# Two feed-forward layers begun at the last block of tokens, one more sweep by seven products, and subtractions lent from VectorE to GpSimd

## The chip, the cores and the metric

One core of a Trainium2 chip runs the whole program. The metric is the device time of one execution in microseconds (us), as the median of the runs. The engines are TensorE (PE; its weight loads are PEld), VectorE (DVE), ScalarE (ACT) and GpSimd (POOL); SyncE (SP) issues nearly all DMA transfers.

## The reference

Windowed attention with a distance bias, then two feed-forward layers on the 2304 tokens:

```python
rel = pos[:, None] - pos[None, :]
scores = scale * np.matmul(q, k.transpose(0, 1, 3, 2))       # 4 x 8 heads, 576 tokens, 64 wide
scores = np.where((rel >= 0) & (rel < 128), scores - slopes * abs(rel), -1e9)
x = softmax(scores) @ v                                       # then 2304 tokens x 512
h = x @ w_in                                                  # 512 x 2048
x = np.where(h > 0, h, np.exp(np.minimum(h, 0)) - 1) @ w_out  # layer 0, ELU
h = x @ w_in2
out = (h / (1 + np.exp(-h))) @ w_out2                         # layer 1, SiLU
```

## The kernel before

**Stages.** Attention runs first, in units of 256 tokens and two heads, and in between them the first sweep of layer 0 (`block_first`, on blocks of 256 or 512 tokens): a sweep is a quarter of the 2048 hidden columns, for both products. The last such block (`block_first(NB - 1)`) stands alone behind the attention, from about 181.5 us on. Then come 21 steps: a step is one layer, one sweep and one of three blocks of 768 tokens. Steps 0 to 8 are sweeps 1 to 3 of layer 0, steps 9 to 20 the four sweeps of layer 1. The results add up in the tiles `acc0` to `acc2`, one a block.

**Precision.** Every operand is held as two float32r tiles, a rounded upper half (ScalarE copies it) and a lower half (VectorE subtracts the upper from the value), and a product is three matmuls: upper by upper, upper by lower, lower by upper.

**Seven products.** The first product of every step (`quad`) takes 2 x 2 blocks by seven products, not eight. Its operands are combinations of x, in the tiles `c0` to `c6`, and of the weights, in `wa` to `wd`. The combinations of x are made by VectorE's `form` operations and the halves, once a block (`make`), are stored to DRAM (`d`) and reloaded (`reload`) in the later sweeps. The results are summed into the tiles `hs` and `h2` (a "sum" is such an instruction), go through the activation in the tiles `e`, `xs`, `t2` and `t3`, and land as upper and lower halves in the tiles `g`. The second product goes by eight products (`outputs`, 96 matmuls of 384 columns a step of layer 0) or by seven (`seven_outputs`, 84), where `BY_SEVEN` lists the layer and sweep; by seven, `seven_activated` forms combinations of the activated tiles and `place` makes their halves, and `y_weight` makes those of the weights `w1` and `yb`.

**Which block comes first.** `ORDER` lists the blocks of each sweep, with block 0 first in sweep 1. Its combinations and those of block 1 are made during the attention (`make_ahead`, through the staging tiles `st`), while those of block 2, whose tokens are attended last, are made during step 1, for step 2.

**The order of the work** is a planner's (`Plan`): every operation has a cost and a latest start worked back from due times, and at build time the planner runs through the program and emits each engine's queue in that order. An engine then works its queue strictly in order. In the planner, VectorE and GpSimd share a port: an operation of the one with all operands in SBUF keeps the other's out, while VectorE's operations on PSUM are free (`port=False`).

```python
    ORDER = ((0, 1, 2), (2, 1, 0), (0, 1, 2)), ((0, 1, 2), (2, 1, 0), (0, 1, 2), (2, 1, 0))
    BY_SEVEN = {(0, 2), (1, 0), (1, 1), (1, 2), (1, 3)}
    HELP = {"place": (0, 1), "lower": (0, 1), "wlow": (0, 1), "c": (0, 1)}
```

By `HELP`, none of each kind of lower half goes to GpSimd, and in the layers it has nothing to do.

Of the kernel before, what the change touches and what calls it, by code (L numbers as in the profile page):

```python
# [13 lines left out]
AF = mybir.ActivationFunctionType  # L14
# [8 lines left out]
def f32(ap):  # L23
    return ap.bitcast(F32)
# [10 lines left out]
class Plan:  # L35
# [14 lines left out]
    def add(self, eng, cost, fn, r=(), w=(), due=1.0e9, moved=0, after=(), floor=0.0, port=None, kind=None):  # L50
        op = Op(eng, cost, fn, due, moved and self.DMA_START + self.DMA_END + moved / self.DMA_RATE or self.DRAIN.get(eng, 0.0), len(self.ops))
        op.moved, op.floor, op.kind = moved, floor, kind
# [84 lines left out]
def attention_elu_silu_kernel(  # L137
# [195 lines left out]

    def split_weight(tag, keys, src, half, w, r, low_eng="DVE"):
# [4 lines left out]
        eng = {"DVE": nc.vector, "POOL": nc.gpsimd}[low_eng]  # L339
        add(low_eng, cost if low_eng == "DVE" else 1.1,  # L340
            lambda: eng.tensor_tensor(T[lo], f32(src()), f32(T[hi]), op=ALU.subtract), r=list(r) + [hi], w=[lo])

# [3 lines left out]
    def y_weight(t):  # L346
# [18 lines left out]
        def form(d, x, y):  # L365
            add("DVE", 0.34, lambda: nc.vector.tensor_tensor(d[0](), x[0](), y[0](), op=ALU.subtract), r=x[1] + y[1], w=d[1])
        src, r = whole(t, 1)
# [10 lines left out]
    def weight(i):  # L378
# [48 lines left out]
        else:  # L427
# [625 lines left out]
    ns = {"hs": 0, "h2": 0, "e": 0, "g0": 0, "g1": 0, "below": 0, "a": 0}  # L1053
    g_of, g_unread = {}, {}
# [12 lines left out]
    vec = {"DVE": nc.vector, "POOL": nc.gpsimd}
    HELP = {"place": (0, 1), "lower": (0, 1), "wlow": (0, 1), "c": (0, 1)}
    helped = {n: 0 for n in HELP}

    def helper(name):
        a, n = HELP[name]
        helped[name] += a
        if helped[name] >= n:
            helped[name] -= n
            return "POOL"
        return "DVE"

    def place(k, q, i, src, sk):
# [46 lines left out]
    def activated(k, f, half, src, sk):  # L1126
# [9 lines left out]
        if layer == 1:  # L1136
            add("ACT", 0.42, lambda: nc.scalar.activation(T[ek], src(), AF.Silu), r=[sk], w=[ek])
            add("ACT", 0.44, lambda: nc.scalar.activation(T[gk[0]], src(), AF.Silu), r=[sk], w=[gk[0]])
        elif slot("below", 2):
            def bent():  # L1140
# [5 lines left out]
            add("ACT", 0.43, lambda: nc.scalar.activation(T[gk[0]], T[ek], AF.Copy), r=[ek], w=[gk[0]])  # L1146
        else:
            add("ACT", 0.42, lambda: nc.scalar.activation(T[ek], src(), AF.Exp), r=[sk], w=[ek])
            add("DVE", 0.28, lambda: clamp(T[ek]), w=[ek])
            add("DVE", 0.475, lambda: nc.vector.tensor_tensor(T[ek], src(), T[ek], op=ALU.max), r=[sk], w=[ek], port=sk[0] != "m")  # L1150
            add("ACT", 0.43, lambda: nc.scalar.activation(T[gk[0]], T[ek], AF.Copy), r=[ek], w=[gk[0]])
        eng = helper("lower")
        add(eng, 0.475 if eng == "DVE" else 1.0, lambda: vec[eng].tensor_tensor(T[gk[1]], T[ek], f32(T[gk[0]]), op=ALU.subtract),
            r=[ek, gk[0]], w=[gk[1]])

# [229 lines left out]
    def layers():  # L1385
# [85 lines left out]
```

## Time and profile before

| | before |
|---|---|
| time, median of 3 runs | 846.22 us (844.97 to 848.49) |
| the profiled execution | 845.84 us, its span 844.1 us |
| TensorE busy | 833.9 us (99%) |
| VectorE busy | 734.9 us (87%) |
| ScalarE busy | 593.5 us (70%) |
| GpSimd busy | 82.3 us (10%), all before 181.5 us |

The profile is of one execution. Busy time is the union of an engine's instructions, which may overlap on VectorE and ScalarE. The stages named above are the reader's clock: attention up to 181.5 us, the block alone to 203.5, steps 0 to 2 to 297.7, steps 3 to 5 to 386, steps 6 to 8 to 480.2, layer 1 to the end.

### The profile page before, as it was taken

How to read it: one execution, taken by the hardware profiler on the slowest of the kernel's cores; microseconds unless marked ns; L12 is line 12 of the kernel's file. 1: busy time of each engine (PE TensorE's matmuls, PEld its weight loads, DVE VectorE, ACT ScalarE, POOL GpSimd, SP SyncE). 2: the span in 40 equal slices, each digit the busy share in tenths (PEclk: the TensorE clock that was granted, in tenths of full speed). 3: DMA queues.
4: the chain of work that ended last, by engine and by line, in shares of the span. 5: the costliest groups of instructions: out<-in, count | busy, mean ns of one | idle time of the engine just before them, and what ended most of it. 6: DMA issues, size and time to landing. Idle time of an engine off the chain costs nothing.

```text
span 844.1 us, 17025 instructions
## 1 busy us (share of the span) xinstructions
PE 833.9 (99%) x6254; PEld 789.7 (94%) x6254; DVE 734.9 (87%) x1753; ACT 593.5 (70%) x1387; POOL 82.3 (10%) x171
## 2 busy tenths in 40 slices
PE   8999999999999999999999999999999999999998
PEld 5788777778999999999999999999999999999998
DVE  8998997955999869999998789999998899798757
ACT  7988987855876666685857588789757566755532
POOL 6254534410000000000000000000000000000000
PEclk9999999999999999999999999999999999999999
DMA  9765876559817265505786846427661458116722
GB/s 303 253 213 171 268 239 200 191 206 384 311 50 294 81 199 208 217 26 174 286 306 237 281 163 267 166 89 242 245 241 51 149 214 310 50 55 246 286 88 76
DMA packets 75267, 169.66 MB, mean 201 GB/s; under 512 B 5040, under 2 KB 55216, under 8 KB 75184
## 3 DMA queue, kind: packets, MB, share of 16 engines
q1 hardware_dynamic: 74608, 168.05, 56.6%
q8 instruction: 49, 0.80, 0.4%
q10 hardware_dynamic: 576, 0.52, 0.2%
q14 instruction: 34, 0.28, 0.1%
HBM read 126.09 MB, written 42.47 MB: 200 GB/s over the span
## 4 chain that ended last, share of the span: by engine, by line
PE 81%; DMA 7%; DVE 6%; ACT 4%; issue 1%; POOL 1%; SPq 0%; POOLq 0%; ACTq 0%; DVEq 0%
PE m L1176 31%; PE m L1332 25%; PE m L1270 9%; PE m L748 5%; PE m L787 4%; PE a L669 2%; PE s L576 2%; DMA raw<-in_moe_w_in_dram 2%; PE t L636 2%; DMA raw<-in_moe_w_out_dram 2%; DMA d<-xs 1%; ACT p L595 1%; DMA xd<-xt 1%; DMA q<-in_q_dram 1%; DMA acc<-xd 1%
## 5 line engine op out<-in xcount | busy, mean ns | idle before, releaser
L1332 PE MATMUL m<-w,g 128*128 128x256 f32 x1512 | 191.3, 282 | 0.1
L1332 PEld LDWEIGHTS m<-w,g 128*128 128x128 f32 x1512 | 188.7, 190 | 0.3 <-DVE acc L1350 0.3
L1270 PE MATMUL m<-g,w 128*128 128x384 f32 x576 | 110.5, 337 | 1.0 <-DVE e L1144 0.4
L1270 PEld LDWEIGHTS m<-g,w 128*128 128x128 f32 x576 | 101.3, 188 | 2.0 <-DVE e L1144 0.7
L1176 PE MATMUL m<-c,wc 128*128 128x384 f32 x504 | 101.1, 335 | 0.0
L1176 PE MATMUL m<-c,wd 128*128 128x384 f32 x504 | 99.5, 336 | 0.5 <-ACT hs L1185 0.5
L1176 PE MATMUL m<-c,wa 128*128 128x384 f32 x504 | 97.5, 336 | 0.0
L1176 PEld LDWEIGHTS m<-c,wd 128*128 128x128 f32 x504 | 87.9, 188 | 1.1 <-ACT hs L1185 1.1
L1176 PEld LDWEIGHTS m<-c,wc 128*128 128x128 f32 x504 | 88.3, 188 | 0.0
L1176 PEld LDWEIGHTS m<-c,wa 128*128 128x128 f32 x504 | 87.1, 188 | 0.1
L1350 DVE TENSOR_TENSOR acc<-m,acc 128x512 f32<-128x512 f32 (+1 forms) x144 | 75.9, 552 | 8.2 <-PE m L1332 7.0
L617 POOL TENSOR_SCALAR p<-p,sums 128x192 f32<-128x192 f32 x112 | 63.9, 588 | 75.4 <-DVE sums L609 42.8
L595 ACT ACTIVATE p<-p,neg 128x192 f32<-128x192 f32 (+1 forms) x144 | 63.0, 443 | 3.4 <-DVE neg L587 3.4
L1189 DVE TENSOR_TENSOR hs<-m,hs 128x384 f32<-128x384 f32 x84 | 46.5, 554 | 19.5 <-PE m L1176 15.8
L1185 ACT ACTIVATE hs<-m 128x384 f32<-128x384 f32 x84 | 40.8, 486 | 30.1 <-PE m L1176 29.6
L1085 DVE TENSOR_TENSOR g<-xs,g 128x384 fp32r<-128x384 f32 x90 | 49.0, 551 | 7.8 <-ACT g L1083 7.5
L1176 PE MATMUL m<-c,wb 128*128 128x384 f32 x252 | 51.1, 337 | 0.5 <-DVE hs L1189 0.5
L1083 ACT ACTIVATE g<-xs 128x384 fp32r<-128x384 f32 x90 | 45.9, 522 | 3.8 <-DVE xs L1113 2.4
L748 PE MATMUL m<-x,w 128*128 128x512 f32 (+1 forms) x240 | 48.4, 353 | 0.0
L787 PE MATMUL m<-g,w 128*128 128x512 f32 (+1 forms) x240 | 47.2, 350 | 0.6 <-DVE ex L764 0.6
L1332 PE MATMUL m<-g,w 128*128 128x384 f32 x252 | 46.5, 336 | 0.0
L748 PEld LDWEIGHTS m<-x,w 128*128 128x128 f32 x240 | 38.5, 189 | 7.4 <-issue 1.0
(198 smaller groups left out, 1529.6 us busy)
## 6 DMA issues: line engine op xcount, KB each, us to landing
c<-d SPq DMA_DIRECT2D x91, 768.0 KB, 7.3
raw<-in_moe_w_in_dram SPq DMA_DIRECT2D x32, 512.0 KB, 6.8
d<-c SPq DMA_DIRECT2D x21, 768.0 KB, 5.5
raw<-in_moe_w_out_dram SPq DMA_DIRECT2D x28, 512.0 KB, 4.1
d<-st SPq DMA_DIRECT2D x19, 384.0 KB, 3.8
k<-in_k_dram SPq DMA_DIRECT2D x16, 384.0 KB, 5.3
d<-xs SPq DMA_DIRECT2D x14, 384.0 KB, 6.0
v<-in_v_dram SPq DMA_DIRECT2D x18, 256.0 KB, 5.1
```

The costliest lines, as they stand in the source:

```text
L595: nc.scalar.activation(dst, dst, AF.Exp, bias=T["neg", u % 4][:, i:i + 1], scale=-1.0, accum_out=T["sm", u % MS][:, e, j:j + 1])
L617: nc.gpsimd.tensor_scalar(dst, dst, T["sm", u % MS][:, e, j:j + 1], 1.0, op0=ALU.mult, op1=ALU.mult)
L748: nc.tensor.matmul(T[m][:, 0:w], a[:, cs], T["x0", b2][:, c, 0:w], start=(c == 0 and x == 0), stop=(c == NKC - 1 and x == 2))
L787: nc.tensor.matmul(T[m][:, 0:w], a[:, cs], b2[:, 0:w], start=(f == 0 and x == 0), stop=(f == FIRST_F - 1 and x == 2))
L1083: add("ACT", 0.42, lambda: nc.scalar.activation(T[hi], src(), AF.Copy), r=[sk], w=[hi])
L1085: add(eng, 0.475 if eng == "DVE" else 1.0, lambda: vec[eng].tensor_tensor(T[lo], src(), f32(T[hi]), op=ALU.subtract), r=[sk, hi], w=[lo])
L1176: nc.tensor.matmul(T[m][:, 0:HALF], a[:, cs], x[:, j, c, :], start=(begin and c == 0 and n == 0), stop=(c == 1 and n == 2), skip_group_che ...
L1185: add("ACT", 0.4, lambda: nc.scalar.activation(T[s], T[m][:, 0:HALF], AF.Copy), r=[m], w=[s])
L1189: add("DVE", 0.475, lambda: nc.vector.tensor_tensor(T[s], T[m][:, 0:HALF], T[s], op=ALU.add), r=[m], w=[s], port=False)
L1270: nc.tensor.matmul(T[m][:, 0:w], l, rr, start=(f == 0 and x == 0), stop=(f == n - 1 and x == 2))
L1332: nc.tensor.matmul(T[m][:, n * w:(n + 1) * w], l, rr, start=(begin and q == 0 and x == 0 and n == 0), stop=(q == nq - 1 and x == 2 and n = ...
L1350: add("DVE", 0.08 + size / 960.0, lambda: nc.vector.tensor_tensor(dst(), src(), dst(), op=ALU.add), r=[m], w=dk, port=False)
```

## The change

The blocks' order begins with block 2, so its combinations are made at once (`make(0)`, ahead of the last `block_first`), are stored, and blocks 0 and 1 are reloaded in steps 1 and 2. For the second half of x there, `make` uses the tiles `e` and `h2` as well as `xs`. Sweep 1 of layer 0 goes by seven in its second product too. And the planner may move a subtraction from VectorE to GpSimd at build time: one that `either` marks with an alternative cost, if GpSimd is free and VectorE has PSUM work to cover it (`lend`). Also, all activations that go by eight in layer 0 now take the form with one VectorE operation; every second one took a clamp and a maximum.

```diff
+    COVER, SLACK, HURRY = 0.9, 2.0, 1.5
...
     def between(self, a, b):
-        return a.tail + self.LINK if a.eng != b.eng or a.moved else 0.0
+        return a.tail + self.LINK if a.eng != b.eng or a.moved or b.alt else 0.0
+
+    def lend(self, queue, now, busy):
+
+        ready = [x for x in queue if max(x[0], x[1].floor) <= now]
+        alts = [x for x in ready if x[1].alt]
+        free = [x for x in ready if not x[1].port]
+        tied = [x[1].late for x in ready if x[1].port]
+        if not alts or not free and busy <= now:
+            return None
+        x = max(alts, key=lambda x: (x[1].late, x[1].n))
+        if max(busy - now, 0.0) + sum(x[1].cost for x in free) < self.COVER * x[1].alt[0]:
+            return None
+        lead = min([x[1].late for x in ready])
+        if x[1].late < lead + self.SLACK or free and min(tied) < min(x[1].late for x in free) - self.HURRY:
+            return None
+        return x
...
+                if port <= now and free.get("POOL", 0.0) <= now and (x := self.lend(queues.get("DVE", ()), now, free.get("DVE", 0.0))):
+                    queues["DVE"].remove(x)
+                    x[1].eng, x[1].cost, x[1].fn, x[1].tail = "POOL", *x[1].alt, self.DRAIN["POOL"]
+                    x[1].alt, x[1].late = None, -1.0e9
+                    queues.setdefault("POOL", []).append((now, x[1]))
...
-    ORDER = ((0, 1, 2), (2, 1, 0), (0, 1, 2)), ((0, 1, 2), (2, 1, 0), (0, 1, 2), (2, 1, 0))
-    BY_SEVEN = {(0, 2), (1, 0), (1, 1), (1, 2), (1, 3)}
+    ORDER = ((2, 0, 1), (1, 0, 2), (2, 0, 1)), ((2, 0, 1), (1, 0, 2), (2, 0, 1), (1, 0, 2))
+    BY_SEVEN = {(0, 1), (0, 2), (1, 0), (1, 1), (1, 2), (1, 3)}
...
+    LEND = {"wlow": 1.4, "form": 0.75, "place": 1.05, "lower": 1.05, "c": 1.05, "s": 1.05}
+
+    def either(name, cost, fn, r, w):
+
+        if name not in LEND:
+            return add("DVE", cost, lambda: fn(nc.vector), r=r, w=w)
+        part = cost / {"wlow": 0.572, "form": 0.34}.get(name, 0.475)
+        return add("DVE", cost, lambda: fn(nc.vector), r=r, w=w, alt=(LEND[name] * part, lambda: fn(nc.gpsimd)))
...
-            if layer == 0:
+            if layer == 0 and c:
+                own_tiles = [("e", i) for i in range(3)] + [("h2", 1)]
+                src = lambda i, j: T[own_tiles[2 * i + j]]
+                sk = lambda i, j: [own_tiles[2 * i + j]]
+                for i in range(2):
+                    for j in range(2):
+                        load(lambda i=i, j=j: nc.sync.dma_start(src(i, j), x_dram[b][:, c + 2 * i, j * HALF:(j + 1) * HALF]), 192 * 1024,
+                             r=[x for x in plan.keys(("xd",)) if x[1] == b], w=sk(i, j))
+            elif layer == 0:
...
-        if again(k):
+        if again(k) and k == 0:
+            for i in (1, 0, 5, 4, 6, 3, 2):
+                store_lanes(layer, b, i, lambda i=i: T["c", i], lambda c, i=i: [ck(i, c, j) for j in range(2)])
+        elif again(k):
...
-        if k in (0, 1, FAR):
+        if k in (1, 2, FAR):
             return "load"
...
         weights_to((0, 0, SWEEPS[0][1][0] + 1))
-        for i in (0, 1, 5, 4, 6, 3, 2):
-            reload(0, i)
+        make(0)
         block_first(NB - 1, None)
```

The planner decides where everything lands, so three places show what became of it. The first is VectorE's queue at the end of the block that stands alone; `g02` and `g03` are its activated tiles, `e00` its buffer, `hs0` the first sum of step 0. Before:

```order
L767 TENSOR_TENSOR g021_112<-e00_96,g020_109 128x512
L726 TENSOR_SCALAR e00_96<-e00_96 128x512
L764 TENSOR_TENSOR e00_96<-m3_2854,e00_96 128x512
L767 TENSOR_TENSOR g031_118<-e00_96,g030_115 128x512
L341 TENSOR_TENSOR w131_3002<-raw0_84,w130_3001 128x512
L1189 TENSOR_TENSOR hs0_2841<-m1_154,hs0_2841 128x384
```

And now, from the first form on, the first 12 of the 23 instructions ahead of that sum:

```order
L1027 TENSOR_TENSOR t3_2854<-xs_2852 128x384
L1027 TENSOR_TENSOR xs_2852<-xs_2852 128x384
L797 TENSOR_TENSOR g021_112<-e00_96,g020_109 128x512
L1027 TENSOR_TENSOR t2_2853<-xs_2852 128x384
L756 TENSOR_SCALAR e00_96<-e00_96 128x512
L794 TENSOR_TENSOR e00_96<-m3_2858,e00_96 128x512
L988 TENSOR_TENSOR c6_2844<-t3_2854,c6_2844 128x384
L988 TENSOR_TENSOR c1_2839<-xs_2852,c1_2839 128x384
L797 TENSOR_TENSOR g031_118<-e00_96,g030_115 128x512
L1027 TENSOR_TENSOR t3_2854<-h21_2848,e1_2850 128x384
L988 TENSOR_TENSOR c0_2838<-xs_2852,c0_2838 128x384
L988 TENSOR_TENSOR c0_2838<-e0_2849,c0_2838 128x384
```

The forms (L1027) and lower halves (L988) of the combinations now stand between the activation's instructions and ahead of the first sum; the first form reads `xs`, so the chain behind it waits for that load.

The second place is SP's queue behind the last store of x (`xd`). Before, the seven reloads, of which three are shown:

```order
L722 DMA xd_83<-xt_140 512x1x256
L858 DMA d_170<-st_151 256x1x384
L1042 DMA c_2834<-d_161 128x1536
L1042 DMA c_2835<-d_162 128x1536
L1042 DMA c_2839<-d_166 128x1536
```

Now:

```order
L752 DMA xd_83<-xt_140 512x1x256
L888 DMA d_170<-st_151 256x1x384
L1018 DMA xs<-xd_83 128x2x768
L1013 DMA e_2849<-xd_83 128x384
L1013 DMA e_2850<-xd_83 128x384
L1013 DMA h_2848<-xd_83 128x384
L1013 DMA e_2851<-xd_83 128x384
L427 DMA raw_86<-in_moe_w_out_dram 128x1024
L427 DMA raw_87<-in_moe_w_out_dram 128x1024
L1000 DMA d_179<-c_2844 256x1x384
```

Five loads of x took the place of the reloads, and behind two loads of weights begin the 14 stores of the combinations, ahead of the reload for step 1.

The third is GpSimd's queue from the end of the attention on, where before there was nothing behind the last scaling of `p`. Now:

```order
L647 TENSOR_SCALAR p2_129<-p2_129,sums_148 128x192 x4
L396 TENSOR_TENSOR raw3_87<-raw3_87,raw2_86 128x256 x2
L1111 TENSOR_TENSOR g111_3021<-xs_2852,g110_3020 128x384
L370 TENSOR_TENSOR w121_3037<-raw1_85,w120_3036 128x512
L370 TENSOR_TENSOR w151_3043<-raw3_87,w150_3042 128x512
L1111 TENSOR_TENSOR g001_3007<-t2_2853,g000_3006 128x384
L370 TENSOR_TENSOR wb21_2833<-raw1_85,wb20_2832 128x256
```

These are placed halves (L1111), halves of weights (L370) and forms (L396) that stood in VectorE's queue before.

## Rows read from the trace of the kernel before

**Rows 1.** The page: span, and busy time of each engine with its instructions.

```profile
span 844.1 us, 17025 instructions
PE 833.9 (99%) x6254; PEld 789.7 (94%) x6254; DVE 734.9 (87%) x1753; ACT 593.5 (70%) x1387; POOL 82.3 (10%) x171
```

**Rows 2.** Stages: from:to, length, busy PE, PEld, DVE, ACT, POOL; PEclk, DMA share, GB/s.

```profile
181.50:203.50 22.00, 22.00 (x99) 18.19 (x98) 11.05 (x19) 10.90 (x19) 0.00 (x0) 1.00 0.83 324
203.50:297.70 94.20, 94.20 (x541) 94.20 (x540) 82.22 (x167) 68.38 (x137) 0.00 (x0) 1.00 0.53 191
297.70:386.00 88.30, 88.30 (x507) 88.30 (x506) 80.60 (x166) 59.70 (x125) 0.00 (x0) 1.00 0.45 155
386.00:480.20 94.20, 92.75 (x525) 91.47 (x523) 83.85 (x173) 64.52 (x128) 0.00 (x0) 1.00 0.78 271
480.20:820.00 339.80, 339.31 (x2385) 338.66 (x2385) 300.55 (x617) 229.30 (x473) 0.00 (x0) 1.00 0.50 182
```

**Rows 3.** The waits of TensorE: total us, times, longest.

```profile
PE m L1270 <- DVE e L1144: 0.4, 1, 0.4
```

**Rows 4.** The chain that ended last: start us, us, what; second products.

```profile
251.81 8.35 PE m L1270 x48
...
317.99 9.39 PE m L1332 x54
```

**Rows 5.** VectorE's timeline in step 6: start us, us, instruction [idle before].

```profile
385.49 0.55 DVE L1189 TENSOR_TENSOR hs<-m,hs 128x384 f32<-128x384 f32 x1
385.95 0.68 DVE L341 TENSOR_TENSOR wc<-raw,wc 128x512 fp32r<-128x512 f32 x1
386.55 0.55 DVE L1339 TENSOR_TENSOR acc<-m,acc 128x384 f32<-128x384 f32 x1
...
387.88 0.42 DVE L437 TENSOR_TENSOR raw<-raw 128x256 f32<-128x256 f32 x1
388.21 0.42 DVE L341 TENSOR_TENSOR wb<-raw,wb 128x256 fp32r<-128x256 f32 x1
```

**Rows 6.** SP's timeline before step 0: start us, us of issuing.

```profile
184.67 0.51 SPq L858 DMA_DIRECT2D d<-st  x1
187.52 3.60 SPq L1042 DMA_DIRECT2D c<-d  x7
```

**Rows 7.** Line L839, the loads acc<-xd of 768 KB, four of them.

```profile
DMA to landing us min/median/max: 5.0/5.6/6.3
```

**Rows 8.** VectorE's timeline at the end of the last first-sweep block.

```profile
193.67 0.69 DVE L764 TENSOR_TENSOR e<-m,e 128x512 f32<-128x512 f32 x1
195.07 0.69 DVE L767 TENSOR_TENSOR g<-e,g 128x512 fp32r<-128x512 f32 x1 [0.70 <-ACT g L766]
...
198.34 0.69 DVE L767 TENSOR_TENSOR g<-e,g 128x512 fp32r<-128x512 f32 x1 [0.70 <-ACT g L766]
```

**Rows 9.** TensorE's timeline: the first products of step 0.

```profile
203.41 2.24 PE L1176 MATMUL m<-c,wa 128*128 128x384 f32 x12
```

**Rows 10.** Line L1042 from 181 to 210 us, the reloads c<-d, eight.

```profile
DMA to landing us min/median/max: 4.3/8.4/13.6
```

**Rows 11.** GpSimd's scalings, lines L400 and L617: duration ns min/median/max, first and last start.

```profile
L400 POOL TENSOR_SCALAR raw<-raw x4: 657/672/772, 12.3 to 24.2; 128x512 f32<-128x512 f32 x4
...
L617 POOL TENSOR_SCALAR p<-p,sums x112: 362/426/1399, 41.8 to 172.5; 128x192 f32<-128x192 f32 x104, 128x128 f32<-128x128 f32 x8
```

**Rows 12.** GpSimd's timeline in the attention phase.

```profile
122.87 1.63 POOL L617 TENSOR_SCALAR p<-p,sums 128x192 f32<-128x192 f32 x4 [3.39 <-DVE sums L609]
126.45 3.00 POOL L617 TENSOR_SCALAR p<-p,sums 128x192 f32<-128x192 f32 x4 [1.96 <-DVE sums L609]
```

**Rows 13.** VectorE's timeline beside the second of these bursts.

```profile
126.81 0.55 DVE L856 TENSOR_TENSOR st<-acc,st 128x384 fp32r<-128x384 f32 x1
127.28 0.70 DVE L856 TENSOR_TENSOR acc<-acc 128x384 fp32r<-128x384 f32 x1
127.90 0.55 DVE L844 TENSOR_TENSOR acc<-acc 128x384 f32<-128x384 f32 x1
```

More of the change, by code (lines that the diff above doesn't have):

```diff
@@ L48, in __init__, with add @@
         self.ops, self.writer, self.readers = [], {}, {}
-    def add(self, eng, cost, fn, r=(), w=(), due=1.0e9, moved=0, after=(), floor=0.0, port=None, kind=None):
+    def add(self, eng, cost, fn, r=(), w=(), due=1.0e9, moved=0, after=(), floor=0.0, port=None, kind=None, alt=None):
         op = Op(eng, cost, fn, due, moved and self.DMA_START + self.DMA_END + moved / self.DMA_RATE or self.DRAIN.get(eng, 0.0), len(self.ops))
-        op.moved, op.floor, op.kind = moved, floor, kind
+        op.moved, op.floor, op.kind, op.alt = moved, floor, kind, alt
         op.port = eng in ("POOL", "DVE") if port is None else port
@@ L332, in raw_keys, with split_weight @@
         return acc_keys(slot[1], slot[2] * 8 * P, (slot[2] + 1) * 8 * P)
-    def split_weight(tag, keys, src, half, w, r, low_eng="DVE"):
+    LEND = {"wlow": 1.4, "form": 0.75, "place": 1.05, "lower": 1.05, "c": 1.05, "s": 1.05}
[4 more added lines that the diff above has]
+        return add("DVE", cost, lambda: fn(nc.vector), r=r, w=w, alt=(LEND[name] * part, lambda: fn(nc.gpsimd)))
+    def split_weight(tag, keys, src, half, w, r):
         hi, lo = [tag[:1] + tag[1:] + (j,) for j in range(2)]
@@ L338, in split_weight @@
         add("ACT", cost, lambda: nc.scalar.activation(T[hi], f32(src()), AF.Copy), r=r, w=[hi])
-        eng = {"DVE": nc.vector, "POOL": nc.gpsimd}[low_eng]
-        add(low_eng, cost if low_eng == "DVE" else 1.1,
-            lambda: eng.tensor_tensor(T[lo], f32(src()), f32(T[hi]), op=ALU.subtract), r=list(r) + [hi], w=[lo])
+        either("wlow" if tag[0] != "w0" else "", cost, lambda eng: eng.tensor_tensor(T[lo], f32(src()), f32(T[hi]), op=ALU.subtract),
+               list(r) + [hi], [lo])
     def seven(layer, f):
@@ L365, in form @@
         def form(d, x, y):
-            add("DVE", 0.34, lambda: nc.vector.tensor_tensor(d[0](), x[0](), y[0](), op=ALU.subtract), r=x[1] + y[1], w=d[1])
+            either("form", 0.34, lambda eng: eng.tensor_tensor(d[0](), x[0](), y[0](), op=ALU.subtract), x[1] + y[1], d[1])
         src, r = whole(t, 1)
@@ L436, in form @@
             def form(d, x, y, op):
-                add("DVE", 0.34, lambda: nc.vector.tensor_tensor(d[0](), x[0](), y[0](), op=op), r=x[1] + y[1], w=d[1])
+                either("form", 0.34, lambda eng: eng.tensor_tensor(d[0](), x[0](), y[0](), op=op), x[1] + y[1], d[1])
             split_weight(("wb", i), None, a22[0], None, w2, a22[1])
@@ L1000, in make @@
                     r=s[1], w=[ck(i, c, 0)])
-                eng = helper("c")
-                add(eng, 0.475 if eng == "DVE" else 1.0, lambda i=i, s=s, c=c, eng=eng: lower_half(T["c", i], c, s[0](), vec[eng]),
-                    r=s[1] + [ck(i, c, 0)], w=[ck(i, c, 1)])
-        if again(k):
+                either("c", 0.475, lambda eng, i=i, s=s, c=c: lower_half(T["c", i], c, s[0](), eng), s[1] + [ck(i, c, 0)], [ck(i, c, 1)])
+        if again(k) and k == 0:
+            for i in (1, 0, 5, 4, 6, 3, 2):
+                store_lanes(layer, b, i, lambda i=i: T["c", i], lambda c, i=i: [ck(i, c, j) for j in range(2)])
+        elif again(k):
             for i in range(7):
@@ L1048, in source @@
             return "same"
-        if k in (0, 1, FAR):
+        if k in (1, 2, FAR):
             return "load"
         return "make" if not any(s[::2] == (layer, b) for s in steps[:k]) else "load"
-    ns = {"hs": 0, "h2": 0, "e": 0, "g0": 0, "g1": 0, "below": 0, "a": 0}
+    ns = {"hs": 0, "h2": 0, "e": 0, "g0": 0, "g1": 0,  "a": 0}
     g_of, g_unread = {}, {}
@@ L1063, in attention_elu_silu_kernel @@
     places, combo, a_of, pending = [(h, i) for h in range(2) for i in range(GS[h])], {}, {}, []
-    wide_open = lambda k: steps[k][0] == 1 or 2 < k < FAR - 2
+    wide_open = lambda k: steps[k][0] == 1 or k < FAR - 2
     A_TILES = [("e", i) for i in range(ES)] + [("xs", i, j) for i in range(2) for j in range(2)] + [("t2",), ("t3",)]
[L1067 to L1077, printed above, removed]
     def place(k, q, i, src, sk):
@@ L1083, in place @@
         add("ACT", 0.42, lambda: nc.scalar.activation(T[hi], src(), AF.Copy), r=[sk], w=[hi])
-        eng = helper("place")
-        add(eng, 0.475 if eng == "DVE" else 1.0, lambda: vec[eng].tensor_tensor(T[lo], src(), f32(T[hi]), op=ALU.subtract),
-            r=[sk, hi], w=[lo])
+        either("place", 0.475, lambda eng: eng.tensor_tensor(T[lo], src(), f32(T[hi]), op=ALU.subtract), [sk, hi], [lo])
     def seven_activated(k, f, half, src, sk):
@@ L1112, in form @@
         def form(d, x, y, op=ALU.subtract):
-            add("DVE", 0.475, lambda: nc.vector.tensor_tensor(d[0](), x[0](), y[0](), op=op), r=[x[1], y[1]], w=[d[1]])
+            either("s", 0.475, lambda eng: eng.tensor_tensor(d[0](), x[0](), y[0](), op=op), [x[1], y[1]], [d[1]])
         form(a22, a21, a22, ALU.add)
@@ L1138, in activated @@
             add("ACT", 0.44, lambda: nc.scalar.activation(T[gk[0]], src(), AF.Silu), r=[sk], w=[gk[0]])
-        elif slot("below", 2):
+        else:
             def bent():
@@ L1146, in activated @@
             add("ACT", 0.43, lambda: nc.scalar.activation(T[gk[0]], T[ek], AF.Copy), r=[ek], w=[gk[0]])
[L1147 to L1154, printed above, removed]
+        either("lower", 0.475, lambda eng: eng.tensor_tensor(T[gk[1]], T[ek], f32(T[gk[0]]), op=ALU.subtract), [ek, gk[0]], [gk[1]])
     def quad(k, q, last):
```

## The prediction

> **What bounds the kernel now.** I read the busy shares first: TensorE is busy for 833.9 of 844.1 us, VectorE for 734.9, ScalarE for 593.5, GpSimd for 82.3 [rows 1]. Then the stages [rows 2]: from 181.5 to 386 us TensorE has no idle time at all and the granted clock is 1.00; from 386 to 480.2 us it idles for 94.20 - 92.75 = 1.45 us, and from there to 820 us for 0.49 us. So the kernel is a row of matmuls without gaps, and only two things can move its end: fewer matmuls, or gaps that a late producer makes. The producer to watch is VectorE: 82.22 of 94.2 us in steps 0 to 2 and 80.60 of 88.3 us in steps 3 to 5 [rows 2], which is already the sweep done by seven. Where TensorE does wait in the layers it is for VectorE, as for tile e of the activation [rows 3].
>
> **The sweep by seven: -6.3 us.** The second products of steps 0 to 2 now go as 84 matmuls of 384 columns a step, not 96. Forty-eight of the old ones take 8.35 us in a piece of the chain without a gap, 54 of the new kind 9.39 us: 174 ns each either way [rows 4]. 3 x 12 x 0.1745 = 6.28 us. The stages agree: three steps by eight last 94.2 us, three by seven 88.3 us [rows 2]. TensorE idles in neither, so all of it comes off the end, if VectorE keeps up.
>
> **What VectorE gets for it.** A step by seven asks VectorE for 50 instructions of 384 elements (6 sums, 8 activations, 8 forms, 14 lower halves, 14 additions to acc) where one by eight asks for about 34, some of them clamps. I cost them by start to next start, since they overlap: 0.46 us for 384 elements (385.49 to 385.95), 0.60 for 512 (385.95 to 386.55), 0.33 for 256 (387.88 to 388.21) [rows 5]. I counted the instructions in VectorE's order from the first sum of a step to the first sum of the next, weights included. For the old kernel this gives 26.2, 26.4 and 26.7 us for steps 3 to 5, 79.3 together, and the trace has 80.60 [rows 2]: the method holds to 2%. For the new kernel, with what GpSimd takes left out, steps 0 to 5 come to 22.1, 28.4, 25.6, 29.5, 25.6 and 25.6 us, 156.8 in all, and TensorE needs 6 x 29.4 = 176.6. On the average VectorE is at 89%, a little under the 91% (80.60 of 88.3) at which the old sweep by seven ran without a gap. But step 3 alone asks for 29.5 of 29.4 us. VectorE idled for 7.7 us in the three old steps, 2.6 a step, much of it waits that no order removes. With these, step 1 is 28.4 + 2.6 - 29.4 = 1.6 us short and step 3 2.7 us, while steps 0, 2, 4 and 5 have from 1.2 to 4.7 us over. If nothing carries over from step to step the price is 4.3 us; if the eight PSUM banks and the placed halves carry all of it, nothing. The old kernel's order asked for 30.0 of 31.4 us in its step 1 by the same count and TensorE did not stop there, so I stand nearer the lower end: **+0.5 us** (0 to 4.3).
>
> **The start of the layers: 0.** The old kernel reloads seven ready combinations. The new one loads the last block's x (one transfer of 768 KB and four of 192 KB) and makes them while TensorE is at the last first-sweep block: 22 more VectorE and 14 more ScalarE instructions between 181.5 and 203.5 us, where VectorE has 11.05 us of work in 22 and ScalarE 10.90 [rows 2]. The old reload left SP at 187.52 us, behind the store of stage st that was issued at 184.67 [rows 6]; I let the x load leave there too, and the same 768 KB of x took 5.0 to 6.3 us in the attention phase [rows 7]: 193.1 us. The four small ones are 0.8 MB more at about 390 GB/s (324 at a share of 0.83 [rows 2]), some 195 us. In the new order the first form stands behind the activation that began at 193.67 [rows 8], thus at 194.3. Behind it come 12 instructions, 8 of 384 and 4 of the old chain (5.9 us), to the second lower half of c0: 200.2 us. c1 is 5 more behind (202.5), c5 at 203.5, c4 at 203.9, c6 at 204.4. TensorE asks for c0 at 203.41 [rows 9], then c1 at 204.45, c5 at 205.5, c4 at 206.5, c6 at 208.6, a product being 6 x 0.1745. Two microseconds are over. The activation's own chain, which VectorE must serve in between, has waits such as that from 194.3 to 195.07 in which the forms fit [rows 8]. By the median of the old reloads, 8.4 us [rows 10], all would be 1.6 us later and still in time; by their worst, 13.6 us behind six others, TensorE would stop for 4.9 us. The x load is the first in its queue, so I take 0 (0 to 4.9). If this cover were gone, the whole making would show: some 20 x 0.46 = 9 us.
>
> The queue behind it: SP now issues 14 stores of 384 KB, and behind them the reload for step 1. 5.5 MB at 390 GB/s from 200.6 us is 14 us, the first reload 2 us more: about 217 us. TensorE's new order asks for that c0 after 14 products and two output groups, 16.8 us into the step, at 220.2. This covers it by 3 us. The old step 2 loses its making; that is no time, since TensorE did not wait there.
>
> **GpSimd's lending: +0.3 us.** 68 subtractions move from VectorE to GpSimd: 9 forms in or just behind the attention phase, 30 in the next seven steps or so, 29 later. They are out of VectorE's sums above. No row has a GpSimd subtraction of two tiles. Its scaling of 512 elements of one tile has a median of 672 ns [rows 11], so 384 of one tile are about 0.5 us and of two up to 1.0; one scaling of 192 lasted 1399 ns beside VectorE [rows 11]. I take 1.0 us (0.5 to 1.4). What does it do to VectorE? Two bursts of four scalings tell: 1.63 us and 3.00 us [rows 12]. In the longer one VectorE ran instructions with both inputs in SBUF, and these took 0.55, 0.70 and 0.55 us [rows 13], so VectorE lost about 0.15 us to four of GpSimd's and GpSimd lost 1.4 us. So it is the lent half that comes late, not VectorE. The lent work is what was due last, but a placed half such as g11 in step 0 stands only about a microsecond ahead of the matmul that reads it. I take +0.3 us for all (0 to 2 as long as VectorE wins); the other possibility is a rival below.
>
> The page GPSIMD Engine Reference of the Trainium skill, Engine selection, speaks against lending: a two-input elementwise operation belongs on VectorE, GpSimd being about 2x slower, and its Key points say that the two share SBUF interfaces when VectorE reads two SBUF inputs. By its 4497 ns for 2048 elements, 384 would be an estimated 0.84 us, and with VectorE held for all of the 30, reckoned as in rival 2 below, the time would be about 860 us. The bursts above bear out the sharing, and show GpSimd as the one that waits.
>
> **Steps 6 to 8: -0.4 us.** Half of their activations lose the clamp, an instruction each on VectorE, and by count VectorE falls from 28.0 and 27.9 to 25.8 and 24.5 us in steps 7 and 8. The 1.45 us of waits there were for VectorE and for weights behind the reloads; I take a quarter of it back (0 to 1.45).
>
> **Sum.** The profiled execution took 845.84 us for its span of 844.1; the median of the runs, 846.22, is 0.4 above it, within their own spread. 845.84 - 6.28 + 0 + 0.5 + 0.3 - 0.4 = 839.96, so 840.0 us, 0.7% under the median. A measurement of this kernel can tell about 0.5%, that is 842.0 or less, or 850.5 or more.
>
> **Rivals.**
> 1. *VectorE becomes the bound in the seven steps and gives back most.* For: step 3 asks for 29.5 of 29.4 us. Against: 89% on the average, and the old sweep at 91% ran gapless. 845.84 - 6.28 + 4.3 = 843.9 us.
> 2. *The two engines' shared path holds VectorE.* If each of the 30 early lent instructions stopped VectorE for its whole 1.0 us, steps 0 to 5 would ask for 156.8 + 30 = 186.8 us, and with its 2.6 us of unavoidable waits a step 202.4, 25.8 over the 176.6 that TensorE gives: 845.84 - 6.28 + 25.8 = 865.4, slower. Against: the stretched burst, in which GpSimd waited and VectorE did not [rows 12, 13]. It decides where a lent instruction costs VectorE more than about 0.5 us: 156.8 + 15.6 + 30 x 0.5 is 10.8 over, which ends at 850.4.
> 3. *The change does not do what it says at the start*: the x loads come as late as the worst reload, TensorE stops 4.9 us before step 0: 840.0 + 4.9 = 844.9. For: the DMA engines are at a share of 0.83 in that stage of the old kernel [rows 2]. Against: seven reloads made it so, and they are gone.
>
> **Chances and range.** The forecast 70%, rival 1 15%, rival 2 7%, rival 3 8%. Rivals 1 and 3 end within 0.5%. So faster 0.70, same 0.23, slower 0.07. The lowest case takes back all idle time of the layers: 845.84 - 6.28 - 1.45 - 0.49 = 837.6, so the range begins at 837.5. It ends at 845.5, behind rivals 1 and 3, and leaves rival 2 out. The likeliest case's own range is 837.5 to 842.
>
> **What will show it.** The second products' matmuls of 384 columns fall by 36 and still take 174 ns; the stage of steps 0 to 2 lasts 88 us, not 94. At the start, no gap before the first product on a c tile, and the x load landing by 194 us. Right on VectorE: its additions and two-tile subtractions keep 0.55 us, GpSimd's lent ones run 0.8 to 2 us. Wrong: gaps of TensorE released by VectorE's g halves or by GpSimd in steps 1 to 4 (rival 1, if VectorE is busy without a pause there; rival 2, if its instructions are stretched to 1 us), or a gap of several us at the first product released by c (rival 3).

## The result, and the profile after

The changed kernel takes **852.92 us** (median of 6 runs, 850.59 to 854.27); the kernel before took 845.15 us beside it (6 runs, 843.92 to 848.49). The ratio is 1.0083, with a 95% interval of 1.0059 to 1.0107: slower by 0.8%, where 840.0 us, faster, was forecast, and outside the range of the forecast (837.5 to 845.5). The profiled execution took 853.19 us, with a span of 851.4.

The page of the changed kernel, the lines of [rows 1]:

```profile
span 851.4 us, 17165 instructions
PE 832.6 (98%) x6218; PEld 783.1 (92%) x6218; DVE 755.7 (89%) x1733; ACT 615.1 (72%) x1433; POOL 163.9 (19%) x239
```

The 36 matmuls are gone (6218 for 6254), the span is 7.3 us longer all the same, and VectorE is busy for 20.8 us more with 20 instructions fewer. Part of that is the added sweep by seven: this is the same row of the changed kernel when nothing is lent (e1 below):

```profile
PE 830.6 (98%) x6218; PEld 784.6 (93%) x6218; DVE 755.0 (89%) x1801; ACT 612.7 (72%) x1433; POOL 82.5 (10%) x171
```

Lending took 68 of 1801 instructions from VectorE, and its busy time did not fall (755.0 and 755.7 us): instructions that were left have become longer. The stages, with the columns of [rows 2]:

```profile
181.50:203.50 22.00, 22.00 (x109) 18.03 (x105) 16.32 (x31) 15.61 (x31) 0.00 (x0) 1.00 0.65 227
203.50:297.70 94.20, 91.62 (x517) 89.79 (x516) 91.64 (x179) 73.51 (x153) 20.30 (x16) 1.00 0.58 210
297.70:386.00 88.30, 86.20 (x489) 85.08 (x488) 85.78 (x169) 66.70 (x136) 23.34 (x17) 1.00 0.51 173
386.00:480.20 94.20, 93.75 (x535) 93.42 (x534) 79.62 (x159) 68.72 (x139) 0.93 (x1) 1.00 0.75 263
480.20:820.00 339.80, 335.46 (x2343) 332.56 (x2342) 300.76 (x586) 225.03 (x464) 29.61 (x25) 1.00 0.49 180
```

TensorE idles for 4.68 us in the second and third, where it had no idle time in [rows 2], and for 4.34 us in the last, where it had 0.49. In its waits the first place belongs to VectorE's lower halves g (total us, times, longest):

```profile
PE m L1350 <- DVE g L1111: 3.9, 4, 1.6
...
PE m L1194 <- ACT hs L1203: 1.5, 3, 1.1
```

The longest of these is in step 2. The timeline of the changed kernel there, all engines, with the lines of ScalarE and some others left out:

```profile
282.09 1.02 DVE L1111 TENSOR_TENSOR g<-xs,g 128x384 fp32r<-128x384 f32 x2
...
282.86 1.13 POOL L1111 TENSOR_TENSOR g<-e,g 128x384 fp32r<-128x384 f32 x1 [6.55 <-ACT g L1110]
283.03 1.38 DVE L1138 TENSOR_TENSOR xs<-xs 128x384 f32<-128x384 f32 x1
...
285.73 0.55 DVE L1138 TENSOR_TENSOR t<-t,t 128x384 f32<-128x384 f32 x1
286.02 1.14 POOL L1111 TENSOR_TENSOR g<-xs,g 128x384 fp32r<-128x384 f32 x1 [2.03 <-ACT g L1110]
286.20 1.37 DVE L1138 TENSOR_TENSOR e<-xs,e 128x384 f32<-128x384 f32 x1
...
287.12 1.62 POOL L370 TENSOR_TENSOR wd<-raw,wd 128x512 fp32r<-128x512 f32 x1
287.50 1.65 DVE L1138 TENSOR_TENSOR e<-e,t 128x384 f32<-128x384 f32 x1
...
289.07 0.55 DVE L1111 TENSOR_TENSOR g<-t,g 128x384 fp32r<-128x384 f32 x1
...
289.68 1.14 PE L1350 MATMUL m<-g,w 128*128 128x384 f32 x5 [1.56 <-DVE g L1111]
...
290.48 1.01 DVE L1357 TENSOR_TENSOR acc<-m,acc 128x384 f32<-128x384 f32 x2
```

A VectorE instruction on two SBUF tiles takes 0.55 us (285.73). The three that begin while GpSimd subtracts take 1.38, 1.37 and 1.65 us, and the first ends 0.4 us behind GpSimd's: held until GpSimd is through, then run. These 2.75 us push back a half that VectorE makes itself, at 289.07, and TensorE waits 1.56 us for it. That was the sign named for rival 2.

It goes the other way too. At other places of the same kernel, GpSimd's timeline, and VectorE's beside the first of its two rows:

```profile
257.90 3.20 POOL L1111 TENSOR_TENSOR g<-xs,g 128x384 fp32r<-128x384 f32 x1 [3.25 <-ACT g L1110]
...
318.99 3.53 POOL L1111 TENSOR_TENSOR g<-e,g 128x384 fp32r<-128x384 f32 x1 [7.27 <-ACT g L1110]
```

```profile
257.80 0.55 DVE L1111 TENSOR_TENSOR g<-t,g 128x384 fp32r<-128x384 f32 x1
258.27 0.55 DVE L1138 TENSOR_TENSOR e<-e,t 128x384 f32<-128x384 f32 x1
...
260.14 1.94 DVE L1357 TENSOR_TENSOR acc<-m,acc 128x384 f32<-128x384 f32 x4
```

GpSimd began 0.1 us after VectorE, and its 1.0 to 1.1 us became 3.20: it ran only once VectorE had turned to additions from PSUM at 260.14. [rows 12, 13] showed this direction alone.

Behind 200 us the trace has 61 GpSimd subtractions. I count as held each VectorE instruction with all operands in SBUF that overlaps one and takes over 0.75 us where 384 elements take 0.55 (0.55 where 256 take 0.40), and sum what it takes beyond: 37 instructions, 28.5 us. (A row of the timeline can stand for several instructions; the count is of the instructions.) In none of the kernels run does such an instruction exceed these limits without a GpSimd subtraction beside it.

### The profile page after: what moved, and what is told of

It reads as the page before. It is cut to its first block, busy times and chain, and to the rows that moved or that the text cites. A ratio compares the mean times of both kernels' runs of the same rounds, so it can differ in the third digit from the quotient of the medians.

```text
span 851.4 us, 17165 instructions
## 1 busy us (share of the span) xinstructions
PE 832.6 (98%) x6218; PEld 783.1 (92%) x6218; DVE 755.7 (89%) x1733; ACT 615.1 (72%) x1433; POOL 163.9 (19%) x239
## 4 chain that ended last, share of the span: by engine, by line
PE 64%; DVE 18%; ACT 8%; DMA 7%; issue 2%; POOL 1%; SPq 0%; POOLq 0%; DVEq 0%; ACTq 0%
PE m L1194 22%; PE m L1350 21%; PE m L778 5%; PE m L817 4%; PE m L1288 4%; DVE g L1111 3%; PE a L699 3%; DMA d<-xs 3%; PE s L606 2%; DMA raw<-in_moe_w_in_dram 2%; PE t L666 2%; DVE c L988 2%; DVE acc L1368 1%; DVE xs L1138 1%; DVE hs L1207 1%
## 5 line engine op out<-in xcount | busy, mean ns | idle before, releaser
L1350 PE MATMUL m<-g,w 128*128 128x384 f32 x504 | 95.6, 338 | 3.9 <-DVE g L1111 3.1
L1350 PEld LDWEIGHTS m<-g,w 128*128 128x128 f32 x504 | 88.3, 188 | 5.7 <-DVE g L1111 3.8
L1368 DVE TENSOR_TENSOR acc<-m,acc 128x256 f32<-128x256 f32 (+1 forms) x144 | 74.1, 546 | 8.1 <-PE m L1350 7.0
L1110 ACT ACTIVATE g<-xs 128x384 fp32r<-128x384 f32 x112 | 57.6, 523 | 21.6 <-DVE xs L1138 19.7
L1111 DVE TENSOR_TENSOR g<-xs,g 128x384 fp32r<-128x384 f32 x98 | 55.4, 574 | 9.8 <-ACT g L1110 9.6
L1288 PE MATMUL m<-g,w 128*128 128x384 f32 x288 | 56.0, 337 | 1.9 <-ACT xs L1124 1.4
L1111 POOL TENSOR_TENSOR g<-xs,g 128x384 fp32r<-128x384 f32 x14 | 20.8, 1485 | 170.2 <-ACT g L1110 143.6
L1288 PEld LDWEIGHTS m<-g,w 128*128 128x128 f32 x288 | 50.8, 188 | 2.5 <-ACT xs L1124 1.8
L1110 ACT ACTIVATE g<-e 128x384 fp32r<-128x384 f32 x84 | 43.2, 523 | 13.4 <-DVE e L1138 12.0
```

The lines of the kernel that those rows point to most:

```text
L1111: either("place", 0.475, lambda eng: eng.tensor_tensor(T[lo], src(), f32(T[hi]), op=ALU.subtract), [sk, hi], [lo])
L1288: nc.tensor.matmul(T[m][:, 0:w], l, rr, start=(f == 0 and x == 0), stop=(f == n - 1 and x == 2))
L1350: nc.tensor.matmul(T[m][:, n * w:(n + 1) * w], l, rr, start=(begin and q == 0 and x == 0 and n == 0), stop=(q == nq - 1 and x == 2 and n = ...
L1368: add("DVE", 0.08 + size / 960.0, lambda: nc.vector.tensor_tensor(dst(), src(), dst(), op=ALU.add), r=[m], w=dk, port=False)
```

## Where the time goes, in all kernels run

To see where each kernel loses, I read from each trace the start of the first `hs` sum of steps 0, 6 and 20. "Held" is the sum just described. "Steps" are us in the one profiled execution, "median" and ratio (to the kernel before, timed in the same batch at 845.15 to 846.08) are of all runs.

| kernel | median us | ratio, 95% interval | steps 0-5 | steps 6-19 | held us |
|---|---|---|---|---|---|
| before | | | 179.7 | 422.8 | |
| after | 852.92 | 1.0083 [1.0059, 1.0107] | 177.9 | 429.5 | 28.5 |
| e1 no lending | 846.89 | 1.0007 [0.9992, 1.0022] | 182.0 | 421.4 | |
| e2 lending, sweep 1 by eight | 855.30 | 1.0096 [1.0061, 1.0130] | 184.3 | 425.9 | 25.2 |
| e3 before, sweep 1 by seven | 857.22 | 1.0129 [1.0105, 1.0154] | 191.4 | 421.7 | |
| e4 new order alone | 845.82 | 0.9996 [0.9981, 1.0012] | 179.7 | 422.2 | |
| e7 e4 with idle subtractions | 855.15 | 1.0113 [1.0096, 1.0130] | 184.7 | 426.6 | 18.5 |
| e8 e1 without additions in sweep 1 | 840.42 | 0.9935 [0.9914, 0.9956] | 173.1 | 421.4 | |
| e9 after, guarded | 842.79 | 0.9966 [0.9953, 0.9980] | 175.2 | 423.7 | 7.9 |
| e10 e2, guarded | 844.26 | 0.9979 [0.9968, 0.9989] | 178.7 | 421.5 | 6.6 |
| e11 e9 without the guard | 856.79 | 1.0106 [1.0084, 1.0128] | 181.5 | 431.8 | 28.8 |
| e12 guard, after's choice | 844.14 | 0.9970 [0.9958, 0.9982] | 175.1 | 424.6 | 12.5 |
| e13 e9, more cover | 843.23 | 0.9954 [0.9939, 0.9970] | 176.7 | 421.8 | 1.9 |
| e14 e7 at half width | 848.04 | 1.0023 [1.0008, 1.0037] | 181.3 | 423.1 | 9.1 |
| e15 e9 up to step 5 | 843.68 | 0.9978 [0.9965, 0.9991] | 176.3 | 423.2 | 2.8 |
| e16 after, lent up to step 5 | 845.94 | 1.0004 [0.9987, 1.0020] | 178.1 | 422.2 | 10.5 |
| e17 after, lent from step 6 | 857.93 | 1.0132 [1.0105, 1.0159] | 186.0 | 424.9 | 23.5 |

What the changed kernel lost against before, by this: steps 0 to 5 gain 1.8 us, steps 6 to 19 lose 6.7, the last step 1.1; the attention phase ends 1.3 us later, but that differs by up to 3.7 us among these kernels (first sum at 205.0 to 208.7 us) and I explain nothing with it.

## The experiments

**The parts apart (e1 to e4).** The theory ("L" below): holding, that is, GpSimd's subtractions stop VectorE. The rival ("S"): the sweep by seven overloads VectorE and lending is harmless. On the new order, lending and the new seven are taken away in turn and together; e3 puts the new seven alone into the kernel before.

```diff
 e1, e4:
-    LEND = {"wlow": 1.4, "form": 0.75, "place": 1.05, "lower": 1.05, "c": 1.05, "s": 1.05}
+    LEND = {}
 e2, e4:
-    BY_SEVEN = {(0, 1), (0, 2), (1, 0), (1, 1), (1, 2), (1, 3)}
+    BY_SEVEN = {(0, 2), (1, 0), (1, 1), (1, 2), (1, 3)}
 e3, in the kernel before:
+    BY_SEVEN = {(0, 1), (0, 2), (1, 0), (1, 1), (1, 2), (1, 3)}
+    wide_open = lambda k: steps[k][0] == 1 or k < FAR - 2
```

> The changed kernel with nothing lent to GpSimd (LEND is empty); order of blocks and the sweep by seven stay. Theory L (a lent subtraction holds VectorE for about 0.8 us, as 38 stretched instructions of 1.2 to 1.7 us in the trace of after suggest, and brings its half late): layer 1 goes back to the pace of before, so steps 9 to 20 lose nothing; the time is 841 to 848, faster than the changed kernel by 5 us or more. Theory S (VectorE has too little time for the sweep by seven, and lending relieves it): steps 0 to 5 get slower by 5 us or more than in the changed kernel, the time is 853 or more.

> The changed kernel with sweep 1 of layer 0 by eight again; order of blocks and lending stay. Theory L: the loss in steps 9 to 13 and at the end is still there, 850 or more. Theory S: the loss was the seven's, so 844 to 847, as before.

> The kernel before with sweep 1 of layer 0 by seven and nothing else (the activated tiles of these steps use the wider set of buffers, as in the changed kernel). Theory L: the 6.3 us of matmuls mostly come off, 840 to 844. Theory S: VectorE is short in steps 0 to 5, 847 or more.

> The changed kernel with neither lending nor the added sweep by seven: the order of blocks, the making at the start and the one-operation activation are left. Both theories: 844 to 847. If the 1.3 us by which the changed kernel is late at the first sum of step 0 is due to the new start or order, it is here too; if to lending in the attention phase, it is gone.

The order alone changes nothing (845.82). Lending adds 9.5 us without the seven (e2 over e4) and 6.0 with it (after over e1, from two batches; 6.4 by the ratios). The seven adds 1.1 us without lending (e1 over e4) and takes 2.4 off with it (after under e2); the intervals overlap in both, and 6.3 off is not among what they allow. So both theories hold a part. In e1 VectorE is the bound of these steps; its stages and its first wait of TensorE:

```profile
203.50:297.70 94.20, 93.24 (x530) 92.28 (x529) 91.84 (x193) 71.66 (x151) 0.00 (x0) 1.00 0.56 197
297.70:386.00 88.30, 84.54 (x466) 82.48 (x465) 83.75 (x175) 64.20 (x133) 0.00 (x0) 0.98 0.48 173
```

```profile
PE m L1350 <- DVE acc L1357: 4.1, 5, 2.1
```

VectorE is at 175.6 of 182.5 us, and TensorE waits for the additions that free its banks. In the old order, where step 1 also makes the combinations for step 2, it is worse; the same wait of e3 (L1339 is its line for these additions):

```profile
PE m L1332 <- DVE acc L1339: 9.1, 6, 5.4
```

So what the new order is worth shows only together with the seven: 857.22 us in the old order (e3), 846.89 in the new one (e1).

**Is VectorE what eats the 6.3 us? (e8)** Without the 42 additions into `acc` in sweep 1, on e1.

```diff
                 lo_c = (2 * cols + tiles[0]) * BIG + rows * HALF
+                if sw == 1:
+                    return
                 add("DVE", ...
```

> The changed kernel without lending (846.9 us, sweep 1 by seven), and without VectorE's additions into acc in sweep 1: 42 instructions of about 0.48 us, 20 us of VectorE. The output then lacks the second sweep's share. If VectorE is the bound of steps 3 to 5 once they go by seven, the saving of the 36 matmuls that was forecast comes back: 839 to 841.5 us. If the matmuls saved are not worth 6.3 us, or something else than VectorE holds these steps (the upper halves on ScalarE, the weights), it stays at 845.5 to 848.

Measured 840.42 us. Steps 0 to 5 take 173.1 us, 6.6 under the kernel before: the 6.28 forecast is there as soon as VectorE keeps up. Its stages have no gap:

```profile
203.50:297.70 94.20, 94.20 (x537) 93.72 (x536) 86.35 (x179) 78.77 (x164) 0.00 (x0) 1.00 0.63 222
297.70:386.00 88.30, 88.30 (x507) 88.30 (x506) 82.46 (x170) 65.01 (x135) 0.00 (x0) 1.00 0.45 161
```

**Late halves or a held VectorE? (e7, e14)** The prediction held that a lent half comes late and VectorE loses nothing. So GpSimd subtracts where the planner would have lent, but into a tile that nobody reads, while VectorE makes every half itself.

```diff
-                    queues["DVE"].remove(x)
-                    x[1].eng, x[1].cost, x[1].fn, x[1].tail = "POOL", *x[1].alt, self.DRAIN["POOL"]
-                    x[1].alt, x[1].late = None, -1.0e9
-                    queues.setdefault("POOL", []).append((now, x[1]))
+                    free["POOL"] = now + x[1].alt[0]
+                    x[1].alt[1]()
+                    x[1].alt = None
...
+            n = min(320, dst.shape[-1])        # e14: 160
+            nc.gpsimd.tensor_tensor(T["spare",][:, 0:n], a[:, 0:n], b[:, 0:n], op=op)
```

> The order of the layers alone (no lending in effect, no seven in sweep 1, 845.8 us), and beside it 43 GpSimd subtractions at the places where the planner would have lent them, 128x320 wide, into a tile of their own that nobody reads. VectorE does all its own work, so no lower half can be late. If what lending costs is VectorE being held while GpSimd subtracts, the time rises: the kernel with lending and no seven had 31 held VectorE instructions of 0.8 us, 25 us in all, and lost 9.5 us, and here VectorE is relieved of nothing in return, so 851 to 862 us. If the lent halves coming late is what costs, it stays at 845 to 847.5.

> The kernel with idle subtractions (855.2 us against 845.8 without them) at half the width, 128x160, so that each takes about half of its 1.08 us. If the time lost is that for which VectorE is held, it falls by half or more: 848 to 851.5 us. If every interruption costs the same however short, 853 to 856.

e7 takes 855.15 us: 9.3 more than e4, for work that nobody needs, and as much as real lending costs (e2, 9.5). No half can be late in it, and behind 205 us no instruction of the other engines waits for GpSimd's by its list of waits, so it is not tiles that GpSimd still reads either. In its timeline, all engines, at the first of these subtractions in the layers:

```profile
316.64 0.93 POOL L363 TENSOR_TENSOR spare<-xs,g 128x320 f32<-128x320 f32 x1 [143.00 <-DMA raw<-in_moe_w_in_dram]
...
316.75 1.24 DVE L1146 TENSOR_TENSOR xs<-t,xs 128x384 f32<-128x384 f32 x1
...
319.08 0.55 DVE L1146 TENSOR_TENSOR t<-e,t 128x384 f32<-128x384 f32 x1
```

At half the width, e14, the same two read:

```profile
316.39 0.58 POOL L363 TENSOR_TENSOR spare<-xs,g 128x160 f32<-128x160 f32 x1 [143.43 <-ACT g L1118]
...
316.50 0.89 DVE L1146 TENSOR_TENSOR xs<-t,xs 128x384 f32<-128x384 f32 x1
```

0.93 us of GpSimd holds VectorE for 0.69 us, 0.58 for 0.34. About as many instructions are held (27 for 30), but held time falls from 18.5 to 9.1 us and the loss from 9.3 to 2.2 us (848.04). So the loss goes with the time for which VectorE is held and not with the number of holds, and about half of that time or more is absorbed.

**Can the holds be placed? (e9 to e13)** The planner lends under cover of PSUM instructions on VectorE, by its own clock. But GpSimd begins when its operands are there. The guard ties the start to VectorE's queue: a one-column memset there, ahead of the PSUM instruction that is to be the cover, and a one-column copy of it on GpSimd ahead of the subtraction.

```diff
-        if not alts or not free and busy <= now:
+        if not alts or not free or busy > now:
             return None
-        if max(busy - now, 0.0) + sum(x[1].cost for x in free) < self.COVER * x[1].alt[0]:
+        if sum(x[1].cost for x in free) < self.COVER * x[1].alt[0]:
...
                     queues["DVE"].remove(x)
+                    self.guard()
...
+    def guard():
+        if ("guard", 0) not in T:
+            return
+        nc.vector.memset(T["guard", 0], 0.0)
+        nc.gpsimd.tensor_copy(T["guard", 1], T["guard", 0])
+    plan.guard = guard
```

e10 is this without the new seven; e11 has the two changed conditions and no guard, e12 the guard and the old conditions; e13 has `COVER` at 1.2 for 0.9.

> The changed kernel, with each lent GpSimd subtraction in the layers made to wait for a one-column VectorE memset that stands in VectorE's queue right before the PSUM instruction that the planner meant as its cover, and lent only when VectorE is about to begin such an instruction: 57 subtractions on GpSimd instead of 64 (those of the attention phase counted). If what costs is that GpSimd begins at another moment than planned and then holds a VectorE instruction on two SBUF tiles, the held time falls from 27 us to under 10 and the time to 842 to 847 us. If the lent halves come too late, or GpSimd's subtractions hold VectorE whatever stands in its queue, 851 us or more.

> The same guard without the seven in sweep 1 (39 subtractions on GpSimd instead of 42). If mistimed holds are what costs, 845 to 848 us instead of 855.3; if the lent halves themselves come late, 853 or more.

> The guarded kernel (842.8 us) without the guard: the same instructions are lent at the same places of the plan, in the same order, but GpSimd begins each as soon as its operands are there. If the guard's binding of GpSimd's start to VectorE's queue is what spared the time, held VectorE time goes back up from 6 us to 18 us or more and the time to 848 to 854 us. If it was the choice of what is lent (only where VectorE is about to begin a PSUM instruction), it stays at 842 to 845.

> The changed kernel with the guard and its own rule of what is lent (also while a PSUM instruction already runs on VectorE): 65 subtractions lent. The guard then stands behind the running instruction, so GpSimd begins up to half a microsecond later than planned. If the guard spares the time, 842 to 847 us; if the choice does, 850 or more.

> The guarded kernel with more PSUM work asked for before a subtraction is lent (1.2 times its time instead of 0.9): 38 lent instead of 57. If the remaining 6 us of held time still cost something, 840.5 to 842.5 us; if the relief of VectorE in steps 3 to 5 is what counts now, fewer lent make it slower, 843.5 to 846.

The guard decides it, not the choice. With it 842.79 and 844.14 us and 7.9 and 12.5 us held, without it 856.79 and 852.92 and 28.8 and 28.5. The timeline of e9 where the changed kernel above had its holds:

```profile
280.62 1.02 DVE L1121 TENSOR_TENSOR g<-xs,g 128x384 fp32r<-128x384 f32 x2
...
284.37 0.56 DVE L1148 TENSOR_TENSOR e<-e,t 128x384 f32<-128x384 f32 x1
284.40 0.06 DVE L229 MEMSET guard<- 128x1 f32 x1
...
285.02 0.55 DVE L1121 TENSOR_TENSOR g<-t,g 128x384 fp32r<-128x384 f32 x1
...
285.80 0.45 POOL L230 COPY guard<-guard 128x1 f32<-128x1 f32 x1 [0.19 <-DVE guard L229]
286.12 0.55 DVE L1148 TENSOR_TENSOR xs<-xs,e 128x384 f32<-128x384 f32 x1
286.21 1.34 POOL L1121 TENSOR_TENSOR g<-e,g 128x384 fp32r<-128x384 f32 x1
286.59 2.88 DVE L1367 TENSOR_TENSOR acc<-m,acc 128x384 f32<-128x384 f32 x6
...
287.50 1.02 POOL L1121 TENSOR_TENSOR g<-xs,g 128x384 fp32r<-128x384 f32 x1
```

GpSimd now subtracts beside the additions from PSUM, and each VectorE instruction on two tiles takes 0.55 or 0.56 us. From the pair of g halves to the additions VectorE needs 5.97 us (280.62 to 286.59) where it needed 8.39 (282.09 to 290.48), for twelve instructions on SBUF tiles either way. e13 has four held instructions left, 1.9 us, and is no faster than e9 (843.23): with 38 subtractions lent, not 57, VectorE keeps more work, and steps 0 to 5 take 176.7 us for 175.2. It lies between its two expectations.

**In which steps does the loss arise? (e15 to e17)**

```diff
+            stage[0] = k
...
-        if name not in LEND:
+        if name not in LEND or not stage[0] <= 5:      # e15 (on e9), e16 (on after); e17: > 5
```

> The guarded kernel with lending up to step 5 only: 28 subtractions lent instead of 57. In the guarded kernel steps 0 to 5 took 175.2 us and steps 6 to 19 423.7, and without any lending the latter took 421.4. If lending pays only where VectorE is the bound, both good parts come together: 842.8 - 2.3 = 840.5 us (839.5 to 842). If the lending of the later steps was harmless there, 842 to 844.

> The changed kernel (no guard) with lending up to step 5 only: 33 subtractions instead of 64. If its loss lies in steps 6 to 19 (429.5 us against 421.4 without lending) and lending still pays in steps 0 to 5 (177.9 against 182.0), 852.9 - 8.1 = 844.8 us (843.5 to 846.5). If the loss comes from the early steps, 850 or more.

> The changed kernel with lending from step 6 on only: 40 subtractions. If the loss lies in the later steps, it has the bad half of both: 846.9 + 8.1 = 855 us (853 to 857). If the loss comes from the early steps, 846 to 849.

Unguarded lending of what steps up to 5 ask for gives 845.94 us, of what steps from 6 on ask for 857.93: the loss is with the later operations. Some of these are early in time, since the weights of step 6 are prepared ahead: in e17, 11 of the 34 held instructions lie between 345 and 391 us, and steps 0 to 5 take 186.0 us. With the early operations alone these steps take 178.1 us (e16), against 182.0 without any lending (e1): by the traces lending pays there even unguarded, where VectorE is the bound; of the medians only 0.95 us of it is left, within their intervals. e15 missed its 840.5: 843.68 us, not better than e9. Its steps 6 to 19 took 423.2 us, not 421.4, so lending is not what costs the last 2 us there; I leave that open.

## Why the prediction was wrong

1. **The sweep by seven: -6.3 us** was right as a saving of TensorE: 36 matmuls fewer, and 6.6 us where VectorE keeps up (e8).
2. **"So it is the lent half that comes late, not VectorE" (+0.3 us)** is the step that failed. Measured: +6.0 us with the seven, +9.5 without. The argument rested on one burst [rows 12, 13], in which GpSimd had come second. In the layers it often comes first, and then VectorE waits for what is left of GpSimd's 1.1 us. Rival 2 named the mechanism and had 7%, but it priced the 30 early instructions alone, at 1.0 us each (865.4). The trace has 28.5 us for all 61, or 0.47 each, below the 0.5 from which it was to decide, and the early ones by themselves cost nothing on balance (845.94 us in e16, 846.89 with none lent). It decided all the same through the instructions lent from step 6 on, for which neither the forecast nor the rival had a price of their own: by themselves they give 857.93 us (e17). The Trainium skill has this on its page SBUF — State Buffer, section SBUF: two separate sides: of a VectorE instruction with two SBUF inputs and a GpSimd one that reads SBUF, whichever starts first gets the shared port pair for the whole instruction and the other fully blocks. At 283.03 and 286.20 the trace agrees; at 257.90 GpSimd waited through a chain of VectorE instructions, not for one.
3. **"What VectorE gets for it" (+0.5, 0 to 4.3)** was counted with the lent work gone and at full speed. Against 179.7 - 6.3 = 173.4 us, steps 0 to 5 are 1.8 us over where lending hardly holds VectorE (e9), 4.5 in the changed kernel, and 8.6 without lending (e1). So the range was right for the premise, and the premise was step 2's. Rival 1 is what remains when lending is taken away: 846.89, where it had 843.9. So of the 12.9 us between forecast and result, 6.9 are there with nothing lent and 6.0 come with the lending. Even with the guard the seven is worth only 1.5 us of the medians (e9 under e10), and 3.5 in steps 0 to 5 of the traces.
4. **The start of the layers: 0** was right. There is no gap in 181.5 to 203.5 us; the x load left at 188.5 and landed 4.9 us later, at 193.4 (forecast 193.1). The first product on a c tile follows the last first-sweep matmuls directly:

```profile
202.82 1.76 PE L817 MATMUL m<-g,w 128*128 128x512 f32 x7
204.41 2.24 PE L1194 MATMUL m<-c,wa 128*128 128x384 f32 x12
```

5. **Steps 6 to 8: -0.4 us**: without lending they take 91.2 (e1) and 92.0 us (e4) where they took 92.4, so -0.4 to -1.2; with lending 93.8.

Shown: that GpSimd's subtractions hold VectorE, that subtractions which do nothing else lose as much time as lent ones, and that binding their start removes the loss. Not settled: why GpSimd gets in at 286.02, in the middle of a VectorE chain, and not at 257.90 or 318.99.

The guarded kernel, 842.79 us at a ratio of 0.9966 [0.9953, 0.9980], is faster than both, by 0.3% than the kernel before and by 1.2% than the changed one (842.79 / 852.92, of two batches). It is still 2.8 us above the forecast.

## What to carry to other kernels

Before work is moved from VectorE to GpSimd, price what each instruction does to VectorE in both orders of arrival, and look for a row of either. A planner's cover on VectorE is worth nothing if the other engine starts on its own; a one-column write in VectorE's queue makes it start there. Where VectorE is not the bound, lending brings nothing, and each hold can still cost.

## What the runs showed of the hardware

- A GpSimd subtraction of two tiles, 128x384, takes 1.02 us undisturbed (287.50 in e9), and up to 3.53 us beside a chain of VectorE instructions on two SBUF tiles (318.99 in the changed kernel).
- A VectorE instruction that comes second is lengthened by nearly all that is left of GpSimd's: 0.55 us becomes 0.89, 1.24 and 1.38 us beside 0.58, 0.93 and 1.13 us.
- The guard is not free: a memset of one column is recorded with 0.06 us, but the next instruction begins 0.65 us after the one before it (284.37 to 285.02), not 0.47, and GpSimd's copy of one column takes 0.18 to 0.50 us.
